# Convolution and transposition of the first two blocks in one banded matmul instead of transposes and diagonal taps

## The chip, the cores and the metric

One core of a Trainium2 chip runs the whole program. The metric is the device time of one execution in microseconds (us); given is the median of three runs. The engines are TensorE (PE in the profile, its weight loads PEld), VectorE (DVE), ScalarE (ACT), GpSimd (POOL) and the DMA queues, of which SP's carries most loads and all stores.

## What is computed

A causal convolution over seven tokens, with one softmax-normalised set of taps for each of eight heads of 24 channels, and then a SwiGLU block:

```
w   = softmax(weight)                         # 8 heads x 7 taps
y[b, s, h, :] = sum_k w[h, k] * x_pad[b, s + k, h, :]   # x is 8 x 4096 x 192
out = (silu(y @ w_gate) * (y @ w_val)) @ w_out          # 192 -> 1536 -> 192
```

All inputs and outputs are float32; the matmuls take float16 operands. 32,768 tokens go through both parts.

## The kernel before

The tokens are cut into 64 blocks of 512 (TB), two blocks to a pair. The 192 channels are held as three groups of 64 (g = 0, 1, 2). Each block runs 12 chunks (NCH) of 128 hidden columns: `Block.first` (L490, L491) makes gate and val by three pairs of matmuls, each pair side by side on the two halves of the array's rows; `Block.gate` applies silu on ACT (L495) and the product on DVE (L497) to give h; `Block.second` (L502) adds the chunks of the block before into `acc`, four units a chunk. PSUM holds two banks for gates, three for vals, one called run and two for acc (L552 to L555). The gates of the chunks named in `PLAN["third"]` use the run bank in block 0.

From pair 1 on, the convolution is not done on TensorE. SP loads x in squares (`emit_load`, L103), DVE transposes them (`emit_turn`, L114), and the taps are added by ACT (L410, L417), DVE (L427) and POOL (L432, L439, L445); the swapped halves come by two DMAs on SP (L393, L394). `PLAN` says at which chunk each of these steps is issued. `todo` holds steps by chunk number, and they are recorded behind the matmuls and the gate of that chunk. Each engine runs its instructions in the recorded order. A marker on SP's queue (`mark`, L387) carries one of TensorE's waits in `second`.

Pair 0 has no time for that and is convolved on TensorE. x is loaded with tokens on the partitions (L127), cast to float16 (L179, L182) and transposed by matmuls against an identity (L247, L249, L255). The taps are softmaxed on 8 partitions (L201 to L212), spread over the channels by small matmuls (L265) and turned into diagonal matrices (L291). `conv_a` (L320) and `conv_c` (L328) then add seven taps as diagonal matmuls of 64 x 64 or 128 x 64 with 256 columns. For channel groups 0 and 1 that is done twice, with the high and the low float16 part of the taps. The sums of block 0 hold the two token halves on the two halves of the partitions; they are copied out (L361, L364), doubled by a matmul (L336) and copied again (L347) into D0, D1 and D2, the operands of block 0's first layer. Block 1's x is transposed in the opening too (xtA1, xtC1), and its three convolutions, `lateA("hi")`, `lateA("lo")` and `lateC`, are issued behind chunks 1, 4 and 7 of block 0. Their results are copied out by ACT (L603, L609) and exchanged by DMA (L600). In the opening TensorE also runs matmuls of zeros (`warm`, L238).

The weights come by POOL's queue in six loads (L143), the output weights by one more (L544).

Of the kernel before, what the change touches and what calls it, by code (L numbers as in the profile page):

```python
# [19 lines left out]
        (None, 1, (2, 3), (1, 2), 2, 3, 14),  # L20
        (18, 20, (22, 23), (21,), 20, 23, 31),
    ),
    gate=2, val=3, lead=4, third=(5, 8, 11),
# [4 lines left out]
def kernel(  # L28
# [11 lines left out]
    fp16 = mybir.dt.float16  # L40
    AF = mybir.ActivationFunctionType
# [83 lines left out]
    x_sb = xpool.tile([P, 2 * SUBS, D], fp32, tag="x_sb", name="x_sb", bufs=1)  # L125
    for lo, hi in ((0, 2), (2, SUBS), (SUBS, 6), (6, 2 * SUBS)):
        nc.sync.dma_start(  # L127
            out=x_sb[:, lo:hi, :],
            in_=x_flat[lo * P : hi * P, :].rearrange("(s p) d -> p s d", p=P),
        )  # L130
    taps = const_pool.tile([H, K], fp32, tag="taps", name="taps")
    nc.scalar.dma_start(out=taps, in_=weight)
# [8 lines left out]
    def load_w(lo, hi, which):  # L141
# [8 lines left out]
    soft = const_pool.tile([H, K + 1], fp32, tag="soft", name="soft")  # L150
    nc.vector.memset(soft[:, K : K + 1], 1e-9)


    mask = const_pool.tile([H, D], fp16, tag="mask", name="mask")
    nc.gpsimd.memset(mask, 1.0)
    nc.gpsimd.affine_select(
        out=mask, in_=mask, pattern=[[1, D]],
        compare_op=ALU.is_ge, fill=0.0, base=0, channel_multiplier=-grp,
    )
    nc.gpsimd.affine_select(  # L160
        out=mask, in_=mask, pattern=[[-1, D]],
        compare_op=ALU.is_ge, fill=0.0, base=grp - 1, channel_multiplier=grp,
    )
    ident32 = const_pool.tile([P, P], fp32, tag="ident32", name="ident32")
    make_identity(nc, ident32)
    ident = const_pool.tile([P, P], fp16, tag="ident", name="ident")
    twin = const_pool.tile([P, 2, DB], fp16, tag="twin", name="twin")
    nc.gpsimd.tensor_tensor(
        twin,
        ident32[:, 0:DB].unsqueeze(1).to_broadcast([P, 2, DB]),  # L170
        ident32[:, DB:P].unsqueeze(1).to_broadcast([P, 2, DB]),
        op=ALU.add,
    )
    twin = twin[:, :, :].rearrange("p t c -> p (t c)")

    x16 = xpool.tile([P, 2 * SUBS, 2 * P], fp16, tag="x16", name="x16", bufs=1)

    def cast_a(copy, lo, hi):
        copy(x16[:, lo:hi, 0:P], x_sb[:, lo:hi, 0:P])  # L179

    def cast_c(copy, lo, hi):
        copy(  # L182
            x16[:, lo:hi, P:].rearrange("p s (t c) -> p s t c", t=2),
            x_sb[:, lo:hi, P:D].unsqueeze(2).to_broadcast([P, hi - lo, 2, DB]),
        )
# [3 lines left out]
    cast_c(nc.gpsimd.tensor_copy, 0, 2)  # L189
    cast_c(nc.gpsimd.tensor_copy, 2, 4)  # L190
    cast_a(nc.gpsimd.tensor_copy, 4, 8)
    cast_c(nc.gpsimd.tensor_copy, 4, 8)
    for b in range(2):
        load_w(4, 8, b)
    for b in range(2):
        load_w(8, NCH, b)


    wmax, wsum = (const_pool.tile([H, 1], fp32, tag=n, name=n) for n in ("wmax", "wsum"))
    raw = const_pool.tile([H, K], fp32, tag="raw", name="raw")  # L200
    nc.vector.tensor_reduce(wmax, taps, axis=AX.X, op=ALU.max)  # L201
    nc.vector.tensor_tensor(raw, taps, wmax.to_broadcast([H, K]), op=ALU.subtract)
    nc.scalar.activation(soft[:, 0:K], raw, AF.Exp)
    nc.vector.tensor_copy(ident, ident32)
# [3 lines left out]
    parts = const_pool.tile([H, 3, K], fp16, tag="parts", name="parts")  # L208
    rest = const_pool.tile([H, K], fp32, tag="rest", name="rest")
    nc.vector.tensor_tensor(parts[:, 0, :], soft[:, 0:K], wsum.to_broadcast([H, K]), op=ALU.mult)  # L210
    nc.vector.tensor_tensor(raw, soft[:, 0:K], wsum.to_broadcast([H, K]), op=ALU.mult)
    nc.vector.tensor_tensor(parts[:, 1, :], raw, parts[:, 0, :], op=ALU.subtract)  # L212
    own = const_pool.tile([H, P], fp16, tag="own", name="own")
    nc.scalar.copy(
        own[:, :].rearrange("h (t c) -> h t c", t=2),
        mask[:, P:D].unsqueeze(1).to_broadcast([H, 2, DB]),
    )
    cast_a(nc.scalar.copy, 0, 2)
    cast_a(nc.scalar.copy, 2, 3)
    cast_a(nc.vector.tensor_copy, 3, 4)  # L220

    opening = ctx.enter_context(ExitStack())
    pool0 = opening.enter_context(tc.tile_pool(name="xts0", bufs=1, space=bass.MemoryType.PSUM))
    early = {
        n: pool0.tile(shape, dt, tag=n, name=n)
        for n, shape, dt in (
            ("xtA0", [P, TB // 2], fp32),
            ("xtA2", [P, TB // 2], fp32),
            ("sumA", [P, 2, TB], fp32),
            ("idle", [P, 2, TB], fp32),  # L230
            ("xtC", [P, DB + TB], fp16),
            ("taps0", [P, TB], fp32),
        )
    }

    def warm(*repeats):
        for r in repeats:
            nc.tensor.matmul(  # L238
                early["idle"][:, 0, 0 : r * P].rearrange("p (r c) -> p r c", c=P), zeros,
                zeros.unsqueeze(1).to_broadcast([P, r, P]), start=True, stop=True,  # L240
            )

    def turn(xt, cols, s0, subs=range(SUBS), hist=False):
        off = 0
        if hist:
            off = DB
            nc.tensor.transpose(xt[:, 0:DB], x16[DB:P, s0 - 1, cols], ident[DB:P, DB:P])  # L247
        for s in subs:
            nc.tensor.transpose(xt[:, off + s * P :][:, 0:P], x16[:, s0 + s, cols], ident)  # L249

    colA, colC = slice(0, P), slice(P, 2 * P)

    def turn_a(s0):
        for k in range(2):
            ins = nc.tensor.matmul(  # L255
                early[f"xtA{s0}"][:, ts(k, P)], x16[:, s0 + k, colA], ident, start=True, stop=True
            )
        return ins
# [3 lines left out]
    taps_ps = early["taps0"][:, 0 : 7 * K].rearrange("p (n k) -> p n k", k=K)  # L262

    def spread(heads, rows, out, some):
        nc.tensor.matmul(taps_ps[rows, out, :], heads, parts[:, some, :], start=True, stop=True)  # L265

    every = slice(0, P)
    warm(*6 * (SUBS,))
    warm(1)
    spread(mask[:, 0:P], every, slice(0, 1), slice(0, 1))  # L270
    warm(SUBS)
    turned = turn_a(0)

    if n_pairs > 1:
        sync_after(nc.sync.nop(), turned, "squares after x")
        for part, _ in PLAN["load"]:
            emit_load(1, part, None if part > 1 else 0)
    turn_a(2)

    xcA, xcC, xcA1 = (  # L280
        const_pool.tile([P, pad + TB], fp16, tag=n, name=n) for n in ("xcA", "xcC", "xcA1")
    )
    nc.vector.memset(xcA[:, 0:pad], 0.0)
    nc.vector.memset(xcC[:, 0:pad], 0.0)

    dg = {n: const_pool.tile([P, K, DB], fp16, tag=f"dg{n}", name=f"dg{n}") for n in ("hi", "lo", "C")}

    def diagonal(d, part):  # L290
        nc.vector.tensor_tensor(  # L291
            d, twin[:, 0:DB].unsqueeze(1).to_broadcast([P, K, DB]),
            part.unsqueeze(2).to_broadcast([P, K, DB]), op=ALU.mult,
        )

    wn = const_pool.tile([P, 2, K], fp32, tag="wn", name="wn")
    diagonal(dg["hi"], taps_ps[:, 0, :])
    spread(mask[:, 0:P], every, slice(1, 2), slice(1, 2))
    spread(own[:, 0:DB], slice(0, DB), slice(6, 7), slice(0, 1))
    spread(own[:, DB:P], slice(DB, P), slice(6, 7), slice(1, 2))  # L300
    warm(2)
    nc.vector.tensor_tensor(rest, raw, parts[:, 0, :], op=ALU.subtract)
    nc.vector.tensor_tensor(parts[:, 2, :], rest, parts[:, 1, :], op=ALU.subtract)
    diagonal(dg["lo"], taps_ps[:, 1, :])
    diagonal(dg["C"], taps_ps[:, 6, :])
    two = const_pool.tile([P, 1], fp32, tag="two", name="two")
    for s0 in (0, 2):
        nc.scalar.copy(xcA[:, pad + s0 * P :][:, 0 : 2 * P], early[f"xtA{s0}"])
    nc.scalar.activation(two, one, AF.Silu)

    TH = TB // 2
    sides = ((slice(0, DB), 0), (slice(DB, P), TH))

    def conv_a(sums, xc, d, first):
        for k in range(K):
            for cols, t0 in sides:
                for g, r in enumerate((slice(0, DB), slice(DB, P))):
                    nc.tensor.matmul(  # L320
                        sums[cols, g, 0:TH], d[r, k, :], xc[r, k + t0 : k + t0 + TH],
                        start=first and k == 0, stop=not first and k == K - 1,
                    )

    def conv_c(bank, xc):
        for k in range(K):
            for cols, t0 in sides:
                nc.tensor.matmul(  # L328
                    bank[cols, 0:TH], dg["C"][:, k, :], xc[:, k + t0 : k + t0 + TH],
                    start=k == 0, stop=k == K - 1,  # L330
                )


    def double(out, fold):
        for half, (r, _) in enumerate(sides):
# [206 lines left out]
    if n_pairs > 1:  # L542
        emit_turn(1, 1)
# [195 lines left out]
```

## Time and profile before

| | us |
|---|---|
| median of 3 runs | 770.63 (770.48 to 771.24) |
| the profiled execution | 770.44 |
| its span | 768.7 |
| TensorE busy | 764.4 (99%) |
| DVE, ACT, POOL busy | 657.4, 658.7, 667.0 |
| first gate matmul of block 0 | 9.95 |
| first gate matmul of block 1 | 21.73 |

The times in the timeline are from the start of the span. A row of the timeline gives start, busy time, engine, line, operation, output and inputs by name, shapes and count; in square brackets stands how long the engine was idle just before, and what released it. Matmul ends are modelled, and a matmul's own duration (0.38 us for 512 columns) is longer than the distance to the next one on the same part of the array (0.215 us), because they are pipelined.

### The profile page before, as it was taken

The numbers are of one execution on the slowest core, as the hardware profiler recorded it, in microseconds if no ns is written. First come the engines' busy times: TensorE is split into PE (matmuls) and PEld (weight loads), VectorE is DVE, ScalarE is ACT, GpSimd is POOL, SyncE is SP. The second block draws the span as 40 slices with busy tenths as digits, with TensorE's granted clock in tenths as the row PEclk, the third lists the DMA queues.
The fourth block names the chain that finished last, engine by engine and source line by source line (L and its number), as shares of the span: only waits on it lengthen the run. The fifth ranks groups of instructions, "written<-read, shape, count | busy, mean of one in ns | idle before, by whom it ended". The sixth has DMA issues, their size and how long they took to land.

```text
span 768.7 us, 28112 instructions
## 1 busy us (share of the span) xinstructions
PE 764.4 (99%) x10955; PEld 510.2 (66%) x10955; DVE 657.4 (86%) x1041; ACT 658.7 (86%) x1190; POOL 667.0 (87%) x643
## 2 busy tenths in 40 slices
PE   9999999999999999999999999999999999999998
PEld 5766666666666666666666666666666666666666
DVE  6888988888888889888888888888888888888875
ACT  7888888888888888888888888888888888888875
POOL 8799998888999888988889988889888899888850
PEclk9999999999999999999999999999999999999999
DMA  9543344434344433444343344334444333443211
GB/s 170 103 89 85 82 85 89 96 82 88 86 89 87 89 89 78 90 89 91 86 85 90 85 88 91 87 80 88 92 88 88 84 88 85 89 94 87 61 48 52
DMA packets 255158, 67.16 MB, mean 87 GB/s; under 512 B 207920, under 2 KB 255024, under 8 KB 255024
## 3 DMA queue, kind: packets, MB, share of 16 engines
q1 hardware_dynamic: 252208, 63.60, 38.4%
q0 software_dynamic: 2800, 1.77, 1.7%
q8 instruction: 85, 1.39, 0.8%
q14 instruction: 49, 0.40, 0.2%
q10 hardware_dynamic: 16, 0.00, 0.0%
HBM read 29.55 MB, written 25.17 MB: 71 GB/s over the span
## 4 chain that ended last, share of the span: by engine, by line
PE 99%; issue 0%; ACT 0%; DVE 0%; SPq 0%
PE gate L490 61%; PE acc L502 32%; PE val L491 4%; PE idle L238 0%; PE acc L690 0%; PE sumA L320 0%; PE acc L320 0%; PE val L690 0%; PE run L690 0%; PE acc L328 0%; PE taps L328 0%; PE xtC L249 0%; PE taps L265 0%; PE xtA L255 0%; PE taps L249 0%
## 5 line engine op out<-in xcount | busy, mean ns | idle before, releaser
L497 DVE TENSOR_TENSOR h<-silu,val 128x512 f16<-128x512 f16 x768 | 509.3, 680 | 100.7 <-ACT silu L495 69.7
L495 ACT ACTIVATE silu<-gate 128x512 f16<-128x512 f32 x768 | 453.3, 594 | 97.5 <-PE val L491 87.5
L439 POOL TENSOR_TENSOR t<-t,t 128x512 f32<-128x512 f32 x310 | 394.1, 1271 | 58.7 <-ACT t L410 34.7
L490 PE MATMUL gate<-xc,w_sb 64*128 64x512 f16 x1116 | 409.7, 376 | 0.0
L491 PE MATMUL val<-xc,w_sb 64*128 64x512 f16 x1116 | 409.7, 376 | 0.0
L502 PEld LDWEIGHTS <-h 64*128 64x128 f16 x6048 | 281.1, 94 | 135.6 <-SPq L387 1.0
L490 PE MATMUL gate<-xs,w_sb 64*128 64x512 f16 x1116 | 360.0, 376 | 0.0
L491 PE MATMUL val<-xs,w_sb 64*128 64x512 f16 x1116 | 360.0, 376 | 0.0
L502 PE MATMUL acc<-wo_sb,h 64*128 64x192 f16 x6048 | 359.1, 243 | 0.2 <-SPq L387 0.2
L490 PEld LDWEIGHTS <-w_sb 64*128 64x128 f16 x2340 | 212.2, 94 | 112.2 <-issue 1.5
L491 PEld LDWEIGHTS <-w_sb 64*128 64x128 f16 x2340 | 208.7, 94 | 1.0 <-issue 0.3
L445 POOL TENSOR_TENSOR xc<-t,aD 128x512 f16<-128x512 f32 x93 | 118.1, 1270 | 7.3
L432 POOL TENSOR_SCALAR t<-xtA,wn 128x512 f32<-128x512 f32 x155 | 106.1, 695 | 5.5 <-DVE xtA L114 5.5
L410 ACT ACTIVATE t<-xtA,wn 128x512 f32<-128x512 f32 x124 | 88.4, 713 | 0.0
L540 ACT COPY o<-acc 128x384 f32<-128x384 f32 x126 | 60.4, 479 | 2.8
L427 DVE SCALAR_TENSOR_TENSOR aD<-xtA,wn,run 128x512 f32<-128x512 f32 x62 | 46.0, 742 | 0.0
L410 ACT ACTIVATE t<-xtB,wn 128x512 f32<-128x512 f32 x62 | 44.3, 714 | 0.0
L432 POOL TENSOR_SCALAR t<-xtB,wn 128x512 f32<-128x512 f32 x62 | 42.3, 694 | 1.3 <-DVE xtB L114 1.3
L417 ACT ACTIVATE run<-xtA,wn 128x512 f32<-128x512 f32 x62 | 42.5, 686 | 0.0
L114 DVE STREAM_TRANSPOSE xtA<-sqA 128x544 f32<-128x544 f32 (+1 forms) x48 | 34.6, 721 | 0.0
L427 DVE SCALAR_TENSOR_TENSOR run<-xtA,wn,run 128x512 f32<-128x512 f32 x31 | 23.2, 750 | 0.0
L427 DVE SCALAR_TENSOR_TENSOR run<-xtB,wn,run 128x512 f32<-128x512 f32 x31 | 23.2, 750 | 0.0
(102 smaller groups left out, 180.6 us busy)
## 6 DMA issues: line engine op xcount, KB each, us to landing
out_dram<-o SPq DMA_DIRECT2D x127, 192.0 KB, 2.0
sqA<-in_x_dram SPq DMA_DIRECT2D x92, 132.0 KB, 2.9
xs<-xc SPq DMA_DIRECT2D x186, 64.0 KB, 2.0
sqB<-in_x_dram SPq DMA_DIRECT2D x96, 68.0 KB, 2.4
headA<-in_x_dram SPq DMA_DIRECT2D x28, 128.0 KB, 2.5
headB<-in_x_dram SPq DMA_DIRECT2D x14, 68.0 KB, 2.1
headB<-in_x_dram SPq DMA_DIRECT2D x14, 64.0 KB, 2.1
x_sb<-in_x_dram SPq DMA_DIRECT2D x4, 192.0 KB, 3.0
```

Of the source, the lines that this page charges most:

```text
L410: mul(parts[-1], *self.tap(k))
L417: nc.scalar.mul(self.aD, *self.tap(0))
L427: nc.vector.scalar_tensor_tensor(out=self.aD, in0=v, scalar=s, in1=run, op0=ALU.mult, op1=ALU.add)
L432: self.product(k, lambda t, v, s: nc.gpsimd.tensor_scalar(t, v, scalar1=s, scalar2=1.0, op0=ALU.mult, op1=ALU.mult), self.parts)
L439: nc.gpsimd.tensor_tensor(self.parts[0], self.parts[0], t, op=ALU.add)
L445: nc.gpsimd.tensor_tensor(xc, self.parts[0], self.aD, op=ALU.add)
L490: nc.tensor.matmul(g, w[0:DB, ca, f], a[0:DB, :], start=(i == 0), stop=(i == 2))
L491: nc.tensor.matmul(v, w[DB:P, cb, f], b[DB:P, :], start=(i == 0), stop=(i == 2))
L495: nc.scalar.activation(s, self.g.pop(j), AF.Silu)
L497: nc.vector.tensor_tensor(h, s, self.v.pop(j), op=ALU.mult)
L502: ins = nc.tensor.matmul(acc, self.h[j][r, ts(s, P)], wo_r[r, j, :], start=first and j == 0, stop=not first and j == NCH - 1, skip_group_c ...
L540: nc.scalar.copy(self.o[:, 2 * half : 2 * half + 2, :], self.acc[:, :, 0:D])
```

## The change

Blocks 0 and 1 no longer transpose x. x is loaded in six overlapping windows a block of 96 tokens, each 85 tokens behind the last (`load_x`); 94 rows are used. For each head a banded matrix T of 94 x 88 holds the seven taps along its diagonals, once for the high and once for the low float16 part of each tap. A matmul with 32 channels of the window as the weights and 85 columns of T gives 32 channels of 85 convolved tokens, already with channels on the partitions. Since 32 channels can touch two heads, the cast copies x into two tiles, one with the channels of the even heads and zeros elsewhere, the other with the odd ones, and both are summed.

T is made from taps that are now loaded for 16 copies of each head on 128 partitions: iotas on POOL and comparisons on DVE make a rotation, a picking matrix and the band; four matmuls repeat the taps along the columns (`repeat`), and DVE multiplies them with the band (`cut_band`).

For block 0 each channel group is summed twice, on the lower and the upper 64 partitions (`doubled`), so that the doubling matmuls and the first copy go. For block 1 the two token halves stand on the two halves of the partitions as before (`halves`), and copying and exchange stay.

What else moves: the tap load goes from ACT's queue to the head of SP's; block 1's x is loaded behind the second `repeat` matmul, ahead of pair 1's squares; the six weight loads are issued partly earlier, partly later, and the output weights behind block 1's casts; the first late convolution moves from chunk 1 to chunk 2; the transpose of pair 1's group 1 moves from ahead of chunk 0 to chunk 3, and its taps from chunks 1 to 3 to chunks 4 to 6; the run bank is used by gates 3, 8 and 11 instead of 5, 8 and 11. The first exponential now reads the loaded taps directly.

The diff, cut to its core:

```diff
-        (None, 1, (2, 3), (1, 2), 2, 3, 14),
+        (3, 4, (5, 6), (4, 5), 5, 6, 14),
...
-    gate=2, val=3, lead=4, third=(5, 8, 11),
+    gate=2, val=3, lead=4, third=(3, 8, 11),
...
+    HALF, STEP, W, NW = TB // 2, 85, 88, 6
+    ROWS, LOADED = W + pad, 96
+    nc.sync.dma_start(out=taps[:, :], in_=weight.unsqueeze(1).to_broadcast([H, P // H, K]))
...
+    load_x(0, 0, 1, pad)
+    load_x(0, 1, 3)
+    load_x(0, 3, NW)
...
+    far = numbers("far", [P, 8, K], [[-1, 8], [1, K]], 8, int32)
+    row = numbers("row", [P, 2, H, 8], [[-8, 2], [-16, H], [-1, 8]], 0)
+    off = numbers("off", [P, W], [[-1, W]], -(K // 2))
+    part8 = numbers("part8", [P, 1], [[0, 1]], 0, int32)
...
+    nc.vector.tensor_reduce(wmax, taps, axis=AX.X, op=ALU.max, negate=True)
+    nc.scalar.activation(soft[:, 0:K], taps, AF.Exp, bias=wmax)
...
+    nc.vector.tensor_tensor(spun, rotate, soft[:, 0:K]..., op=ALU.mult)
+    nc.vector.tensor_reduce(turned, spun, axis=AX.X, op=ALU.add)
...
+    for lo, hi in ((0, 3), (3, NW)):
+        cast(nc.scalar.copy, 0, 0, lo, hi)
+        cast(nc.gpsimd.tensor_copy, 0, 1, lo, hi)
...
+    def repeat(part, h0):
+        return nc.tensor.matmul(
+            bank[0:ROWS, 0 : HH * W], left[:, 0:ROWS],
+            pick[:, part, h0 : h0 + HH, :].unsqueeze(2).to_broadcast([P, HH, W // 8, 8]),
+            start=True, stop=True,
+        )
+    def cut_band(part, h0):
+        nc.vector.tensor_tensor(T[0:ROWS, part, h0 : h0 + HH, :], bank..., band..., op=ALU.mult)
+    def convolve(bank, quarters):
+        for part in range(2):
+            for e in range(2):
+                for n in range(len(quarters[0][1])):
+                    for a, (block, windows, t0) in enumerate(quarters):
...
+                        nc.tensor.matmul(
+                            bank[32 * a : 32 * a + 32, out],
+                            x16[0:ROWS, e, win, 32 * block : 32 * block + 32],
+                            T[0:ROWS, part, h, u0 : u0 + out.stop - out.start],
+                            start=part + e + n == 0, stop=part + e == 2, skip_group_check=True,
+                        )
+    warm(6)
+    repeat(0, 0)
+    first = repeat(1, 0)
+    sync_after(nc.sync.nop(), first, "block 1's x after block 0's")
+    load_x(1, 0, NW)
...
+    def doubled(g):
+        convolve(early[f"sum{g}"], [(2 * g + a % 2, range(NW), 0) for a in range(4)])
+    doubled(0)
+    nc.scalar.copy(D0, early["sum0"])
...
+    doubled(1)
+    nc.vector.tensor_copy(D1, early["sum1"])
+    doubled(2)
...
+    for e in range(2):
+        cast(nc.gpsimd.tensor_copy, 1, e, 0, NW)
...
-    at_chunk(1, lambda: lateA("hi"))
-    at_chunk(4, lambda: lateA("lo"))
+    at_chunk(2, lambda: lateA(0))
+    at_chunk(4, lambda: lateA(1))
     at_chunk(4, outA)
     at_chunk(7, lateC)
```

## The prediction

> **What bounds the kernel now.** I read the page first: busy time by engine, then the chain that ended last.
>
> ```profile
> span 768.7 us, 28112 instructions
> PE 764.4 (99%) x10955; PEld 510.2 (66%) x10955; DVE 657.4 (86%) x1041; ACT 658.7 (86%) x1190; POOL 667.0 (87%) x643
> ...
> PE 99%; issue 0%; ACT 0%; DVE 0%; SPq 0%
> ```
>
> The reader is to see that TensorE is the chain from end to end. The change touches only the opening and block 0 (the stages by window show 40 us of TensorE in 40 us from 60 to 100 us, and nothing there is edited). So the result is the time at which block 1 starts, plus waits just behind it. The second view is the timeline of that stretch.
>
> ```profile
> 1.44 1.28 ACT L203 ACT_TABLE_LOAD   x1 [1.44 <-PEq L723]
> ...
> 4.13 0.62 DVE L291 TENSOR_TENSOR dghi<-twin,taps 128x448 f16<-128x448 f16 x1
> ...
> 9.95 0.38 PE L490 MATMUL gate<-D,w_sb 64*128 64x512 f16 x1
> ...
> 10.95 0.74 DVE L114 STREAM_TRANSPOSE xtB<-sqB 128x544 f32<-128x544 f32 x1 [0.46 <-DMA sqB<-in_x_dram]
> ...
> 11.44 1.09 ACT L495 ACTIVATE silu<-gate 128x512 f16<-128x512 f32 x2 [0.70 <-PE gate L490]
> ...
> 11.74 0.96 PE L320 MATMUL acc<-xcA,dghi 64*64 64x256 f16 x28
> ...
> 12.07 1.29 DVE L497 TENSOR_TENSOR h<-silu,val 128x512 f16<-128x512 f16 x2 [0.38 <-ACT silu L495]
> ```
>
> To be seen: the first gate matmul at 9.95, the first silu at 11.44, the first h at 12.07, and one of block 1's three late convolutions at 11.74. The third view is the timeline cut to 11.74-11.76 and to 11.87-11.90.
>
> ```profile
> 11.74 0.30 PE L320 MATMUL acc<-xcA,dghi 64*64 64x256 f16 x4
> ```
> ```profile
> 11.74 0.41 PE L320 MATMUL acc<-xcA,dghi 64*64 64x256 f16 x8
> ```
>
> Four matmuls on four parts of the array start within 20 ns, and four more add 0.41-0.30 = 0.11 us: that is 256 columns at 2.4 a ns and 2.5 ns more (in single records 109 ns).
>
> **The opening.** All 28+28+14 tap matmuls of block 0, the 18 transposes and the 6 doubling matmuls go. In their place come four matmuls of 352 columns, four DVE cuts into T, and three sums of 96 matmuls. I follow the chain of releases.
>
> POOL first makes four iotas, which no row shows. The nearest is the affine select of 128x128 (0.29); the ends are the memset (0.20) and the two-input operation of 128x128 (0.53). I take 0.29: they are done at 2.0 (1.7 to 3.0). Eight small DVE operations at 0.08 apart, or 0.18 where one needs the last (reduce, reciprocal, product at 2.98, 3.16, 3.35), follow to about 3.3. Beside this the tap load, now first on SP, lands near 2.2, as the one on ACT's queue did (wmax at 2.20). The order of instructions shows that the table load of 1.28 now waits for it: 3.5 instead of 2.73. That hides the iotas, up to 0.3 us of error. Exp takes 0.21: 3.8. Then spun, turned, reciprocal, high and left hang on each other, with wsum and full between: 5.1. The first matmul of 352 columns is near 0.31 (256 took 0.28); with 0.11 to reach DVE the first cut starts at 5.5. Cuts come each 0.44: L291 takes 448 elements in 0.62 at a pitch of 0.54, and these have 352. They end at 6.0, 6.5, 6.9 and 7.3.
>
> A group of the new sum is four matmuls on four column strips with some 85 columns: 85/2.4 + 2.5 = 38 ns, if the rule of the third view holds. 96 matmuls are 24 groups, 0.91 us. No row has four strips of 32 columns or so few columns: the ends are 38 ns and the 109 ns shown, and I take 38, since the loads (25 ns for 64 columns, by the first matmul's 293 against 268 ns) are shorter still for 32. Sum 0 runs 6.1 to 7.0, sum 1 to 7.9, sum 2 to 8.8. The two tap matmuls and two changes of the array's shape (0.09 each, between L491 and L320 at 11.66) make the first gate 9.1 instead of 9.95. Casts of x (0.4 to 0.6 each, by L179 and L182) are done before 6.1 if the third load lands by 5.1, as the third of before did. The copies to D0 and D1 (0.59, 0.68) end near 7.9 and 8.8; the gate weights landed at 8.3 and 9.2 and are issued 1 us earlier now. The silu waits for four pairs at 0.215, the last D2 half and one more pair: 10.5 instead of 11.44, so h starts at 11.1 instead of 12.07.
>
> **Late convolutions.** Each of the three cost 7 x 0.109 plus two shape changes and one load: 0.98 (11.66 to 12.64). Now each is 48 matmuls, 12 groups: 0.46 + 0.19 = 0.65. That is 1.0 us less of TensorE. With 109 ns it would be 1.5 each.
>
> **What is late next.** That 1.0 us is not simply won. A block 0 chunk is only 0.645 us of TensorE, but 0.61 of DVE and 0.49 of ACT before any tap. Before, the transpose of sqB ran in a DVE hole ahead of the first h (10.95), and late convolution 1 filled TensorE's wait for the first silu. Now the transpose (0.61 at its pitch) stands behind h3, the two DVE taps (0.65 each) and three ACT taps (0.62 each) come at chunks 4 to 6, and the first late convolution stands behind chunk 2. I wrote block 0 out engine by engine, in order, with these pitches, two gate banks, three val banks and the run bank. TensorE then waits 0.6 us at chunk 2 (for the first silu's bank) and 0.9 at chunk 7: its bank waits for silu 5, which stands behind the fold copy (0.49) and the first ACT tap, both after the second late convolution. Some 0.5 follows at chunks 8 to 11. The last gate of block 0 ends at 20.95; the same working for before gives 21.17 (the trace: 21.4, so it is short by 0.2). So block 0 gains 0.2 to 0.3 in all, of an opening 0.85 earlier and convolutions 1.0 shorter.
>
> One stall may go. At 24.55 TensorE waits for a marker on SP, which is behind eight load issues of 0.53:
>
> ```profile
> 24.90 0.20 PEld L502 LDWEIGHTS <-h 64*128 64x128 f16 x6 [0.47 <-SPq L387]
> ```
>
> Those issues follow the last late convolution, which now ends 1.2 us earlier while block 1 starts only 0.25 earlier: 0.35 off (between 0 and 0.36). On SP the tap load and block 1's own x (442 KB, issued near 5.7) are put ahead of the squares, so these move 1.3 us later: sqB to about 12.5, used after h3 at 13.3; sqA to about 19.5, used after h9 at 20.5. On POOL the output weights are issued 1.7 us later and landed at 19.1 before; they are needed near 20.7. All three have under 2 us of cover.
>
> **Sum**: 770.44 (profiled execution, 768.7 span) - 0.25 - 0.35 = 769.85. The median is 0.19 above that execution: **770.0**.
>
> **Rivals.** *The groups don't get shorter.* If a group of four lasts 109 ns whatever its columns, each sum is 2.6 us, the first gate comes at 9.1 + 3 x 1.7 = 14.2 and the late ones cost 1.5 each; block 0 ends near 28, **777**, slower. For it: no row shows more than one matmul each 27 ns sustained (4 in 109). Against it: starts 3.5 ns apart in a group. It decides from about 50 ns a group on. The Trainium skill (TensorE: Matmul & The Clock Gate, "Wait — 56ns, not 53.3ns?") states that start-to-start never drops below about 25 ns however few the columns; by that 96 matmuls take 2.4 us and the sum is near 776. The trace's 3.5 ns inside a group speaks against it across strips, but a stream of more than 28 matmuls at such a rate is not shown.
>
> *The opening's chain is longer.* Iotas at 0.53, block 1's x landing after 10 us (its first late convolution is reached at 11.1 and needs a POOL cast of 0.69), or a clock still at half in the sums (the seven warm-ups take 2.85 us for 3,200 columns, half rate; TensorE would now stand idle from 3.6 to 5.1): each adds 1 to 2.5 us, **771.5 to 773.5**. The clock was full by 5.1 before, with no such hole.
>
> *The gain is kept whole.* If the waits at chunks 2 and 7 are filled as before: -0.85 - 1.0 - 0.35, **768.4**. Against it: the pitches of ACT and DVE above. That the change does less than it says is excluded by the order of instructions: 288 and 144 small matmuls stand in it.
>
> **How the numbers follow.** Forecast (769.2 to 771.2) 0.46; longer chain 0.27; groups not shorter 0.13; whole gain 0.14. The range 768.3 to 774.5 leaves out the 777 and a few tails. What a measurement tells from no change is about 0.2%, 1.5 us: below 769.1 lie the whole gain and the forecast's low tail, 0.17; within, most of the forecast and the mild end of the longer chain, 0.50; above 772.2, 0.33.
>
> **What would show it.** First gate at 9.1, first silu 10.5; 24 groups in 0.91 us; late convolutions of 0.65; TensorE waits at chunks 2 and 7 with ACT as releaser; no wait for SP at 24. A sum of 2.4 us or more, or a first gate after 10.5, proves me wrong.

## The result and the profile after

The changed kernel takes 781.58 us (median of 4 runs, 780.58 to 782.37) against 770.66 before: ratio 1.014, 95% interval 1.0122 to 1.0157. The forecast was 770.0, with a range from 768.3 to 774.5, so both the size and the sign were missed. The profiled execution is 781.83 with a span of 780.0, 11.3 more than before. The page of the changed kernel, in the lines shown of the page before:

```profile
span 780.0 us, 28650 instructions
PE 766.9 (98%) x11222; PEld 531.1 (68%) x11222; DVE 658.4 (84%) x1049; ACT 657.3 (84%) x1186; POOL 665.8 (85%) x644
...
PE 97%; ACT 1%; SPq 1%; issue 1%; DMA 0%; DVE 0%; ACTq 0%
```

TensorE is still the chain, but 13 us of the span are now outside it instead of 4, and 2% of the chain belong to ACT and SP's queue. The timeline of the changed kernel tells where:

```profile
0.74 0.81 SPq L131 DMA_DIRECT2D taps<-in_weight_dram  x1
...
1.51 0.12 POOL L174 IOTA part<- 128x1 int32 x1
...
4.30 0.16 DVE L221 TENSOR_REDUCE wmax<-taps 128x1 f32<-128x7 f32 x1 [1.41 <-DMA taps<-in_weight_dram]
4.34 1.28 ACT L222 ACT_TABLE_LOAD   x1 [4.34 <-DMA taps<-in_weight_dram]
...
7.39 0.53 PE L277 MATMUL hiA<-pick,left 128*94 128x352 f16 x1 [3.65 <-DVE left L237]
...
7.95 0.52 DVE L285 TENSOR_TENSOR T<-hiA,band 94x352 f16<-94x352 f32 x1 [0.62 <-PE hiA L277]
...
9.57 3.77 PE L302 MATMUL sum<-T,x 94*32 94x85 f16 x211
...
16.96 1.59 PE L302 MATMUL sum<-T,x 94*32 94x85 f16 x77 [3.62 <-issue]
...
18.65 0.60 PE L472 MATMUL gate<-D,w_sb 64*128 64x512 f16 x1
...
21.00 1.08 ACT L477 ACTIVATE silu<-gate 128x512 f16<-128x512 f32 x2 [2.03 <-PE gate L472]
21.63 1.28 DVE L479 TENSOR_TENSOR h<-silu,val 128x512 f16<-128x512 f16 x2 [2.10 <-ACT silu L477]
...
23.04 0.71 PE L302 MATMUL acc<-T,x 94*32 94x85 f16 x48
...
25.77 0.74 DVE L114 STREAM_TRANSPOSE xtB<-sqB 128x544 f32<-128x544 f32 x1
```

The first gate comes at 18.65, after 9.95 before: 8.7 of the 11.3 us. Of the two rows of the sum, the second is the one to read: TensorE stands idle from 13.18, when its next group of four matmuls was due, to 16.96, in the middle of sum 1, with nothing named that ended it ("issue"). That is 3.78 us; the 3.62 of the row counts from a modelled end. Its operands, T and x, were there, since sum 0 has used them. The other 2.6 us lie behind the first gate; the last of them is the marker on SP:

```profile
36.12 0.28 PEld L484 LDWEIGHTS <-h 64*128 64x128 f16 x8 [1.06 <-SPq L369]
```

TensorE waits 0.94 here (35.19 to 36.13) instead of 0.36.

The hole has one more clue. Beside data, the DMA engines carry the engines' own code; the DMA view of the changed kernel lists it as a queue called instruction (q8). This is the view of 14.25 to 15.6:

```profile
DMA packets 489, 0.27 MB, mean 203 GB/s; under 512 B 268, under 2 KB 488, under 8 KB 488
...
q0 software_dynamic: 234, 0.23, 102.9%
q1 hardware_dynamic: 254, 0.03, 28.8%
q8 instruction: 1, 0.02, 5.7%
```

One packet of 16 KB, from 14.30 to 15.53, among 488 packets of data (q0 are POOL's loads, q1 SP's). Over the whole kernel these packets recur once for 256 instructions of TensorE, weight loads counted too: 87 packets for 2 x 11,222 instructions. In the steady state one starts when about 256 k - 64 instructions are done (1,216 at 37.38, the packet at 37.36), and serves the block behind the next 256. In the opening, 192 are done at 10.99 (this is called the crossing below), the packet starts 3.3 us later, and the windows view (columns: window, its length, busy time and count of PE, PEld, DVE, ACT, POOL, granted clock, DMA share, GB/s) shows where TensorE had got to:

```profile
0.00:13.30 13.30, 8.66 (x223) 5.32 (x224) 5.66 (x30) 4.70 (x8) 6.91 (x19) 1.00 0.71 126
13.30:16.90 3.60, 0.05 (x7) 0.00 (x0) 0.61 (x1) 0.00 (x0) 0.00 (x0) 0.93 1.38 193
16.90:18.60 1.70, 1.64 (x79) 1.50 (x78) 0.00 (x0) 0.01 (x1) 0.35 (x1) 0.50 0.96 116
```

223 matmuls and 224 weight loads, 447 instructions (448 is 192 + 256; the list of single records has 449). The 7 in the second row are matmuls whose modelled ends reach into it. In the third row the granted clock is down to 0.50.

**Theory (code):** small matmuls use up instructions faster than their code comes, and its block stood behind data in the DMA engines. **Rivals:** (data) the hole waits for something of sum 1, its operands or its bank; (clock) it is the half clock that costs the time.

### The profile page after: what moved, and what is told of

Its sections match the earlier page's. It is cut to its first block, busy times and chain, and to the rows that moved or that the text cites. A ratio compares the mean times of both kernels' runs of the same rounds, so it can differ in the third digit from the quotient of the medians.

```text
span 780.0 us, 28650 instructions
## 1 busy us (share of the span) xinstructions
PE 766.9 (98%) x11222; PEld 531.1 (68%) x11222; DVE 658.4 (84%) x1049; ACT 657.3 (84%) x1186; POOL 665.8 (85%) x644
## 3 DMA queue, kind: packets, MB, share of 16 engines
q0 software_dynamic: 2800, 1.77, 1.7%
## 4 chain that ended last, share of the span: by engine, by line
PE 97%; ACT 1%; SPq 1%; issue 1%; DMA 0%; DVE 0%; ACTq 0%
PE gate L472 57%; PE acc L484 32%; PE val L473 6%; PE sum L302 1%; SPq L103 1%; DMA taps<-in_weight_dram 0%; ACT silu L477 0%; PE acc L674 0%; ACT L222 0%; PE acc L302 0%; SPq L584 0%; ACT t L392 0%; PE val L674 0%; PE run L674 0%; PE idle L264 0%
## 5 line engine op out<-in xcount | busy, mean ns | idle before, releaser
L484 PEld LDWEIGHTS <-h 64*128 64x128 f16 x6048 | 291.5, 94 | 125.3 <-SPq L369 1.3
L484 PE MATMUL acc<-wo_sb,h 64*128 64x192 f16 x6048 | 364.4, 243 | 0.8 <-SPq L369 0.8
```

What stands on the lines that cost most here:

```text
L484: ins = nc.tensor.matmul(acc, self.h[j][r, ts(s, P)], wo_r[r, j, :], start=first and j == 0, stop=not first and j == NCH - 1, skip_group_c ...
```

## The experiments

Ratios are to the kernel before, with 95% intervals.

**1. Sixteen small matmuls more, ahead of the opening.** They make 32 instructions and no data that anyone waits for.

```diff
+    tiny(16)          # each a matmul of 32 columns of zeros
     warm(6)
```

> The changed kernel with 16 tiny zero matmuls (32 columns) ahead of its warm-ups, so 32 more TensorE instructions before the sums. Code-fetch theory: TensorE runs out of loaded instructions after 448 of them, so its 3.8 us hole follows the 195th small matmul instead of the 211th, and ends near 17 us again; time 781 to 782.5. Data theory (the hole is a wait for an operand or a bank): the hole stays behind the 211th small matmul.

Measured: 782.01, in a single execution. The windows view of this run:

```profile
0.00:12.90 12.90, 8.38 (x223) 4.99 (x224) 5.80 (x29) 4.70 (x8) 6.92 (x19) 1.00 0.62 120
12.90:17.40 4.50, 0.01 (x3) 0.00 (x0) 0.69 (x1) 0.00 (x0) 0.00 (x0) 0.78 1.43 196
```

Again 223 + 224: the hole stays at the same count and so moves to another place of the program, 16 matmuls of the sum earlier. (data) falls.

**2. The first block of code pulled early.** Ninety small matmuls in place of the six warm-ups.

```diff
-    warm(6)
+    tiny(90)
```

> The changed kernel with its six warm-ups replaced by 90 tiny zero matmuls (32 columns), 168 instructions more, all done before 5 us. Code-fetch theory: the 192nd instruction runs near 4.5 us instead of 11.0, the next block of code lands by some 9 us, and no hole of more than 1 us follows the 448th instruction (which is now the 127th small matmul or so); without the hole the clock is full when block 0 starts; 775 to 777. Data theory: the hole stays behind the 211th small matmul, 781 to 782.

Measured: 783.03, ratio 1.0161 (1.0146 to 1.0176). The time was missed. The mechanism held for the first block: its packet came at 6.99 and there is no hole at 447. (182 instructions were done by then, so the count of 192 is not sharp.) I had not thought of the next block. There is a hole a block further, by the windows view:

```profile
0.00:14.10 14.10, 9.05 (x351) 7.60 (x352) 6.41 (x30) 4.71 (x8) 6.91 (x19) 1.00 0.70 127
14.10:18.30 4.20, 0.05 (x7) 0.00 (x0) 0.09 (x1) 0.00 (x0) 0.00 (x0) 0.84 1.38 169
```

351 + 352 = 703, 256 more. The second packet started at 15.78.

**3. Twenty warm-ups in place of six**, so that TensorE does not stand idle before the sums.

```diff
-    warm(6)
+    warm(20)
```

> The changed kernel with 20 warm-ups of 512 columns instead of 6, which fill TensorE's time until the taps are there (3.3 to 7.4 us). Code-fetch theory: sum 0 and 1 run at full clock (39 ns a group, 0.94 us a sum instead of 1.8), the hole comes some 1.5 us earlier but ends at the same landing of code, so the time stays within 1 us: 780.5 to 782. Clock theory (the half clock in the sums is the main loss): 777 to 779.

Measured: 781.21, ratio 1.0136 (1.0121 to 1.0152). The sums ran at 39 ns a group instead of 72, the count of 223 + 224 was reached at 10.6 instead of 13.2, and the hole grew to 5.35 us. (clock) falls as the cause of the total: 2.6 us saved ahead of the hole become 1.0 behind it (16.96 to 15.97) and nothing that can be measured at the end. The run takes away the half clock ahead of the hole only; behind the hole it is there as before.

**4. The tap load on ACT's queue**, as before the change.

```diff
-    nc.sync.dma_start(
+    nc.scalar.dma_start(
         out=taps[:, :],
```

> The changed kernel with the tap load on ACT's queue, as before the change, SP's queue starting with x. Theory that SP's queue order is the cost: the taps land by 2.8 us instead of 4.3 and x 0.9 sooner, repeat starts 1.5 to 2 us earlier; of that the code fetch takes back some: 779.5 to 781.5. Theory that 128 rows of 28 bytes are the cost on whichever queue: the taps still land near 4, only x is 0.9 sooner, 781 to 782.

Measured: 782.92, ratio 1.0153 (1.0136 to 1.017). That is above the ranges of both my cases. The taps came later still, as the timeline of this run has it:

```profile
5.10 0.16 DVE L221 TENSOR_REDUCE wmax<-taps 128x1 f32<-128x7 f32 x1 [2.21 <-DMA taps<-in_weight_dram]
```

So SP's queue is not what delays them. Their 128 packets of 28 bytes ran from 2.21 to 4.49 here, beside x's, and from 2.27 to 3.93 in the changed kernel.

**5. and 6. Fewer instructions.** The low part of the taps is left out of the sums of blocks 0 and 1, which is a third of those sums' work; run 6 also has the twenty warm-ups.

```diff
-        for part in range(2):
+        for part in range(1):
...
-    warm(6)
+    warm(20)          # run 6 only
```

> The changed kernel without the low part of the taps in the sums of blocks 0 and 1: that third of these sums is left out of the computation, so each sum has 64 matmuls in place of 96 and the opening issues about 320 TensorE instructions in place of 510. Code-fetch theory (TensorE runs dry after about 448 instructions because the next block of its code has not come yet): the opening ends before 448, so there is no hole; first gate near 12.5 instead of 18.65, time 773 to 774.5, of which about 0.5 is the work left out of block 1's sums and 1 the work left out of block 0's. Rival (the hole is a wait for data or for the banks at the third sum): a hole of 3 us or more stays ahead of the third sum, first gate at 17 or later, time 779 to 780.

> As the run without the low part (the same third of the sums is left out), with twenty warm-up matmuls in place of six, so that TensorE does not stand idle before the sums. Code-fetch theory: about 335 instructions before the first gate, no hole, and the sums at full clock: first gate near 11.3, 1 us or so earlier than without the extra warm-ups, time 772 to 773. Rival (half clock in the opening costs nothing because the first gate waits for x or for a silu anyway): the time is that of the run with six warm-ups within 0.3.

Measured: 775.87, ratio 1.0069 (1.0052 to 1.0085), and 776.02, ratio 1.0072 (1.0057 to 1.0087). In run 5 there is no hole in the sums and the first gate starts at 12.88, as (code) said; in run 6 it starts at 10.68. But the times are 1.4 and 3.0 us above the ranges that I gave for (code), and 2.2 us at the first gate are worth nothing at the end: the rival named ahead of run 6, the time of run 5 within 0.3, came true. The clock is no longer the reason: the windows view grants 1.00 from 13.7 to 31 in run 5 and from 6 to 31 in run 6. The timeline of run 6 shows what came instead:

```profile
16.77 0.37 PE L473 MATMUL val<-D,w_sb 64*128 64x512 f16 x1 [1.31 <-issue]
...
18.72 0.74 DVE L114 STREAM_TRANSPOSE xtB<-sqB 128x544 f32<-128x544 f32 x1 [2.34 <-DMA sqB<-in_x_dram]
...
19.56 0.69 ACT L399 ACTIVATE run<-xtB,wn 128x512 f32<-128x512 f32 x1 [1.22 <-DVE xtB L114]
```

The code hole is back in block 0 (15.30 to 16.77, at 223 + 224 once more). Then DVE and ACT stand behind a transfer: sqB lands at 18.7, the tap on ACT waits for it, the silus queue behind that tap, and TensorE waits 1.87 (18.95 to 20.82) for a silu's bank. At SP's marker it waits 2.15 more. A shorter opening ran ahead of the squares, which SP issues at 8.55 and 11.08 instead of 4.80 and 6.92.

**7. The new chunk numbers alone, in the kernel before.**

```diff
-        (None, 1, (2, 3), (1, 2), 2, 3, 14),
+        (3, 4, (5, 6), (4, 5), 5, 6, 14),
...
-    gate=2, val=3, lead=4, third=(5, 8, 11),
+    gate=2, val=3, lead=4, third=(3, 8, 11),
...
-        emit_turn(1, 1)
...
-    at_chunk(1, lambda: lateA("hi"))
+    at_chunk(2, lambda: lateA("hi"))
```

> The kernel before with nothing but the new chunk numbers: pair 1's steps at the changed kernel's chunks, block 1's first late sums at chunk 2 instead of 1, the third block's start 3 instead of 5, and the transposition of pair 1's second group no longer in the opening. By the waits that the changed kernel shows at these chunks (0.61 at chunk 2, 0.89 at chunk 7, and the 0.94 mark stall against 0.36) it is slower by 0.5 to 1.5: 771 to 772. Rival (these waits belong to the late opening, not to the chunk numbers): 770.6 within 0.3.

Measured: 771.57, ratio 1.0013 (1.0004 to 1.0023): about 1 us of the loss belongs to the schedule. TensorE waits 0.43 (12.31), 0.58 (17.99) and 0.63 at the marker; the first gate came at 10.61 instead of 9.95 in this profile, which the chunk numbers do not explain.

**8. and 13. Why the code came late.** Run 8 releases block 1's x and pair 1's squares only after the third sum; run 13 releases POOL's second pair of weight loads there too, so that nothing but code is moved between 10 and 15 us.

```diff
-    sync_after(nc.sync.nop(), first, "block 1's x after block 0's")
-    load_x(1, 0, NW)
...
+    last = doubled(2)
+    sync_after(nc.sync.nop(), last, "block 1's x after block 0's")
+    sync_after(nc.gpsimd.nop(), last, "weights after the sums")   # run 13 only
+    load_w(4, 8, 0)                                               # run 13 only
+    load_w(4, 8, 1)                                               # run 13 only
+    load_x(1, 0, NW)
...
```

> The changed kernel with the loads of block 1's x and of pair 1's squares released only after the third sum's matmuls instead of after the second repeat. It asks why the code block came 3.3 to 3.9 us after it was asked for. If the loads stand ahead of it in the queues: the fetch starts within 1.5 us of the crossing of 192 executed instructions (by 12.5 instead of 14.3) and TensorE resumes before 15.5. If the lag has nothing to do with them: fetch at about 14.3 and TensorE resumes at 17. Time not of interest, since the squares come later: 779 to 784.

> The changed kernel with every transfer that was issued between 8 and 18 us (the second part of the gate and value weights, block 1's x, pair 1's squares) released only after the third sum's matmuls. If the code block is late because it stands in the DMA engines behind that data: its fetch starts within 1 us of the crossing of 192 executed instructions (before 12.2, against 14.3), and the hole ahead of the rest of sum 1 is under 1.5 us, against 3.78. If the lag has another cause: fetch at 13.4 or later as with SP's loads alone moved (13.43), hole over 2.5. The weights and x now come too late for the chunks behind, so the time says nothing: 781 to 788.

Measured in run 8: fetch at 13.43 and a hole of 2.79, between my two cases. In run 13 the packet started at 11.84, 0.68 after the crossing at 11.16, and the hole is 0.99. The DMA view of run 13 from 11.8 to 13.3, and its timeline:

```profile
DMA packets 1, 0.02 MB, mean 11 GB/s; under 512 B 0, under 2 KB 0, under 8 KB 0
...
q8 instruction: 1, 0.02, 5.8%
```
```profile
9.74 3.92 PE L300 MATMUL sum<-T,x 94*32 94x85 f16 x211
...
14.48 0.93 PE L300 MATMUL sum<-T,x 94*32 94x85 f16 x77 [0.81 <-issue]
...
15.49 0.39 PE L474 MATMUL gate<-D,w_sb 64*128 64x512 f16 x1
```

Between 10.4 and 11.8 the engines move nothing at all. Alone in them, the packet takes no less time (1.40 us; 1.23 in the changed kernel), but it starts almost at once; TensorE goes on 1.24 after its end. So most of the lag comes with the data in the engines. How full they are does not settle it alone: in the kernel before, POOL's loads alone (q0) take 109% of the 16 engines' time from 10.2 to 11.4, and the packet of 10.32 starts only 1.63 after its crossing at 8.69. Why the lag is twice that in the changed kernel stays open.

The first gate of run 13 is at 15.49 instead of 18.65. The two single executions took 782.66 and 782.39: the data held back are late for block 0. In run 13 TensorE waits 2.7 for block 1's x (to 21.11), and the granted clock is 0.50 from 20.3 to 27.1. So the time itself is no gain.

**9. Run 6 with room for the squares**: group 1 two chunks later, pair 2's square loads behind the marker. A third of the sums is left out as in run 6.

```diff
-        (3, 4, (5, 6), (4, 5), 5, 6, 14),
+        (5, 6, (7, 8), (6, 7), 7, 8, 14),
...
-            at_chunk(max(base + c, 8), lambda q=q, part=part: emit_load(q, part))
+            at_chunk(max(base + c, 14), lambda q=q, part=part: emit_load(q, part))
```

> The run without the low part and with twenty warm-ups (its computation: a third of the sums of blocks 0 and 1 is left out), with pair 1's second group two chunks later (transposition at chunk 5, start at 6) and pair 2's first square loads no earlier than chunk 14, behind the mark on SP's queue. Theory of the late squares: of its 5.5 us over the kernel before, the 1.87 at the silu that stands behind the wait for sqB and the 2.15 at the mark go, so 772 to 773. Rival (those waits move to other places, because the data themselves come later for everything): 775.5 to 776.5.

Measured: 776.82 (775.45 to 778.49), ratio 1.0084 (1.007 to 1.0098). My theory of a cure fell. The rival, that the waits move elsewhere, held, though the time is 0.3 above its range: both waits went, and one of 3.2 us came (21.23 to 24.42) at the run bank, which a gate of block 0 shares with the taps; 1.24 for the code (16.62) and 1.2 for block 1's x stayed. The new wait brought the half clock back (granted 0.50 from 23.62 to 30.45). The profiled execution is the slowest of the four, 1.7 above the median, so the others have less of this. In the waits view of this run (total, times, longest):

```profile
PE gate L472 <- DVE aD L409: 3.0, 1, 3.0
```

**10. and 11. The loads ahead of SP's marker**, moved behind it by the second edit of run 9 alone, in the changed kernel and in the kernel before.

> The changed kernel with pair 2's first square loads no earlier than chunk 14, so that 2.1 us of issues leave SP's queue ahead of the mark. If the mark is late because of them: its 0.94 stall goes and the time is 780.5 to 780.9. If not: 781.6 as it was.

> The kernel before with the same one number changed. If the mark's stall of 0.36 is owed to the issues ahead of it on SP: it goes and the time is 770.1 to 770.3, a little below both kernels. If the loads that come later cost as much elsewhere: 770.5 or above.

Measured: 781.66, ratio 1.0144 (1.013 to 1.0158), and 770.43, ratio 1.0 (0.9991 to 1.0009). The stall at 35.19 went as expected, and with it nothing: TensorE waits 0.49 for the next marker at 41.2 and 0.47 at 45.7 for an exchanged half (xs). In the kernel before the stall of 0.36 went and one of 0.40 came at 30.67. No version beats the kernel before.

**12. The first weights later**, behind POOL's memsets and mask.

```diff
-    load_w(0, 4, 0)
-    load_w(0, 4, 1)
     mask = const_pool.tile([P, D], fp16, tag="mask", name="mask")
...
     nc.gpsimd.memset(parity(x16[:, 1, :, :], 0), 0.0)
+    load_w(0, 4, 0)
+    load_w(0, 4, 1)
```

> The changed kernel with the first two weight loads issued after POOL's memsets and mask (near 2.9 instead of 1.6), so that nothing but x shares the DMA engines with the taps. If the weights are what makes the taps land near 4.2 instead of 2.2: the first DVE operation on the taps comes before 3.8, and the first repeat before 6.9 instead of 7.39. If it is the taps' own 128 rows of 28 bytes: 4.1 to 4.5 as it was. The code hole stays in both, after 449 executed instructions; time 780 to 782.

Measured: 782.02, ratio 1.0142 (1.0125 to 1.0159). The first operation on the taps is at 3.95 instead of 4.30, between my two cases: the weights cost the taps 0.35 of 2.1 us. Their own 128 packets of 28 bytes still run from 2.27 to 3.56 (in the changed kernel to 3.93); before, 8 packets ran from 1.77 to 1.85. The sums started 0.34 earlier, the code came 1.3 later, and the hole grew to 5.10.

## Why the prediction was wrong

**The step that failed** is the sum of the opening: sums "6.1 to 7.0, sum 1 to 7.9, sum 2 to 8.8", first gate at 9.1. It came at 18.65. The 9.55 us between are:

- 3.78: the hole. The forecast had no term for TensorE's own code, that is, it put it at nothing. The sums bring 576 instructions within 3 us, more than two blocks; block 0 had about 220 instructions in its whole opening before, and the next block was fetched at 10.32 and needed at 18.3. Runs 1, 2, 5 and 13 show it.
- 2.27: sums of 4.97 us without the hole, instead of 2.7. A group lasts 72 ns until 12.95 and 39 from there; after the hole 72 again. The forecast had this under the longer chain ("a clock still at half in the sums"), as a possibility. Run 3 shows the 39 ns and also that removing it alone brings nothing.
- 2.3: `left` done for the first matmul at 7.39 instead of 5.1. The tap load "lands near 2.2" was wrong: I took the landing time of another shape, 8 rows, for 128 copies of 28 bytes. The first use is at 4.30 and moves the table load by the same amount.
- 1.2 between that and the sums (2.2 instead of 1.0); in run 3, at full clock, it is 1.16 in all, so about 1.0 of it is the clock too.

Had the taps come in time, x would have been next. The forecast had the casts of x done before 6.1, if the third load landed by 5.1. The first cast waits for x until 7.45, and the last ends at 8.47. Two of the three loads took 5.3 and 5.5 us, where 3.0 was the median before; in run 12, with the first weights behind them, all three took 2.7 to 3.1 and the casts ended near 6.45.

These four parts add up the first gate, not the whole time. In run 5 there is no hole; in run 6 the hole is down to 1.5, the clock is full and the first gate starts at 10.68, 0.7 later than in the kernel before. A third of the sums is left out in both, and still the times are 5.3 and 5.5 above that kernel: the squares and the marker are the next limits. No run took all of these away together, so what the banded sums would take then stays open.

**The groups** were right: 38 ns forecast, 38 to 39 in single records at full clock, over 49 groups in a row. The Trainium skill (TensorE: Matmul & The Clock Gate, "Wait — 56ns, not 53.3ns?") puts the least start-to-start distance near 25 ns; four matmuls on four column strips in 39 ns, 9.7 each, do not keep to it, so the rule does not hold across strips here. The rival that I priced at 777 for it had the sign right by a mechanism that isn't there.

**Right in place and size:** the iotas (done at 1.63; 2.0 forecast), the cuts (pitch 0.44 to 0.57 against 0.44), the late convolutions (0.65 at full clock, as forecast), and the wait at chunk 7 (0.89; 0.9). At chunk 2 it is 0.61 against a forecast of 0.6 if the pitch of a pair is taken as 0.215; with the 0.43 that pairs have there, at half clock, only 0.40 is waiting, so this agreement is in part luck. I expected the gain of the convolutions to be given back by these waits, and run 7 puts about 1 us on the new schedule.

**Wrong, smaller:** SP's marker, where I took off 0.35 and 0.58 were added. The cause I gave, load issues ahead of it, is right for that one stall but not for the time: in runs 10 and 11 the wait came back at a later place. What sets the sum of these waits was not settled. And sqB at 12.5: it is issued at 8.59 instead of 6.1, and landed at 18.7 in run 6.

**Behind the first gate** 2.6 us were lost net, with the late convolutions shorter by 0.3 each. About 1.9 of it is the clock: nine gate and val pairs of block 0 are about 0.427 apart instead of 0.215. The marker and the schedule are the rest; they overlap, so I do not split it further.

The longer-chain rival (771.5 to 773.5) named the clock, which is behind two of the four parts (2.27 and about 1.0; forecast were 1 to 2.5), but neither the taps nor the code. It never let one feed the next: with the taps late TensorE stands idle and the sums begin at half clock, and behind the code hole the clock is at half again.

## What to carry to other kernels

Count instructions, not only their durations: a change that puts 292 small matmuls in the place of 94 at the start of a kernel can run ahead of its own code. Look at the instruction queue in the DMA view, and at whether loads stand ahead of it there; 256 instructions in less time than a block needs to come are a hole, wherever the stream is cut; here it was 6 us from the crossing to the restart (10.99 to 16.96). Do not take such a hole for the whole loss before you have seen what waits behind it. And take a transfer's landing time only from one with as many rows.

## What the runs showed that I had not expected

- TensorE's code came in 16 KB packets, one for 256 instructions. In ten kernels (the changed one, runs 1, 3, 4, 6, 8, 9, 10, 12 and 13) the hole stands behind 449 records, whatever matmul is next: one of sum 1 mostly, one of block 0's val in runs 6 and 9.
- In the versions of the changed kernel with all loads under way, a packet started 3.2 to 5.0 us after its crossing, in run 8 2.3, in run 13, with the engines empty, 0.68; TensorE went on 1.2 to 1.6 us after the packet's end.
- The half clock is not in the granted-clock column ahead of 13 us: the first clock record of the trace is at 12.98, and the column takes the time before it as full, while groups take 72 ns until 12.95. From there records and rows agree: half from 16.39 to 23.22. The hole of 3.78 and those of 4.4 to 5.4 us were followed by gate pairs 0.43 apart, the one of 0.99 by groups of 39 ns and pairs 0.22 apart. The sums were at full rate 3.4 us after they began. The Trainium skill (TensorE: Matmul & The Clock Gate, "What's actually happening") states both a fall to half after about 3.4 us of idleness and a return after about 3.4 us of work; the second agrees with 9.57 to 12.95. The first does not quite: in run 8 a hole of 2.79 was followed by groups of 73 ns within 0.2 us.
